# A local-attention and three-way-maximum MLP kernel: chunks of rows in another order, tap sums of two chunks on TensorE, and a new opening list

## The chip, the cores and the metric

The kernel runs on one core of a Trainium2 chip. The core has five engines that run beside each other, each in its own program order: TensorE (PE in the profile; its weight loads are PEld), VectorE (DVE), ScalarE (ACT), GpSimd (POOL) and SyncE (SP), which in this kernel issues every DMA. The metric is the device time of one execution in microseconds (us). One profiled execution gives the trace; times inside it are counted from the start of its span.

## The reference

Inputs are x (8 x 4160 x 192), weight_gen (8 x 4160 x 8 heads x 7 taps), w1, w2, w3 (192 x 768) and w_out (768 x 192), as 64-bit words for the four matrices. With S positions in a sequence:

```python
w = exp(weight_gen - max over taps); w = w / (sum over taps + 1e-9)
x_pad = 6 zero rows, then x                       # for each of the 8 sequences
attn[s, h] = sum over k of w[s, h, k] * x_pad[s + k, h]      # 24 columns for a head
h = max(max(attn @ w1, attn @ w2), attn @ w3)
out = h @ w_out
```

All float32. Each position needs the six rows before it in its own sequence; at the start of a sequence these are zeros.

## The kernel before

The 33280 positions lie on 128 partitions, 260 consecutive positions (t) on each; a sequence fills 16 partitions. A chunk is four values of t, so 4 x 128 = 512 positions, and there are 65 chunks. A chunk at t = a needs the rows a - 6 to a + 3, so the chunks at t = 0 and t = 4 need rows that belong to the partition before; these come first in this kernel, as chunks 0 and 1. Chunks are loaded in groups ("supers": chunk 0, chunk 1, then threes), by `load_super`: one DMA for the tap weights (wt) and one for the rows (xt), with two buffers of each. Where rows of the partition before are needed, the load is three DMAs, and `clear` on VectorE or `clear_by_dma` (a copy out of a stretch of zeros in `ident`) wipes the rows that a first partition of a sequence must not see.

For each chunk:

- softmax over the taps (`softmax`, L195), once for a super.
- `product` (L220): for each of its four t, GpSimd multiplies seven shifted rows by their weights into r (128 x 192 x 7, taps innermost, three buffers).
- `total` (L240): VectorE adds the seven taps into acc.
- `transpose` (L251): acc is turned so that the 192 columns lie on partitions. For the first three chunks (ON_TENSOR) TensorE does it, with two transposes for each t, into PSUM; for all others VectorE and ScalarE.
- `parts` (L277): the turned x is split into a high part in TensorE's fast 32-bit format and the remainder: xa_hi, xa_lo (columns 0 to 127) and xb, xc (columns 128 to 191 and their remainder).
- `up` (L323): the three products with w1, w2, w3 for six blocks of 128 hidden columns. One matmul uses half of the array's rows (64 partitions), and two streams, "half 0" and "half 1", run on the two halves beside each other. After half 0 of a step SP gets a `nop` that waits for it, and half 1 of the same step waits for that nop (L320, `after`): SP is a relay, in its program order between its DMAs.
- `maximum` (L341): ScalarE copies the first product to m, VectorE takes the maximum with the other two, ScalarE makes h_hi and GpSimd h_lo = m - h_hi.
- `down` (L370): h times w_out, four pieces, one chunk late; the output DMA follows.

The matrices arrive as 64-bit words and are turned into 32-bit high and low parts by `split`, in units a0 to a5 (rows 0 to 127 of w1, w2, w3, two blocks of hidden columns at a time), b0 to b2 (rows 128 to 191) and d0 to d2 (w_out). For a b unit a copy with exchanged partition halves is needed too ("the swap", L566): for b0 and b1 by two DMAs each from wb_hi to wb_hi, for b2 by ScalarE. Blocks 0 and 1 of the hidden columns need b0, blocks 2 and 3 need b1.

The order of the opening is a table, OPENING: at each tick (22 ticks are a chunk) a list of stages, such as x0.3 (product of chunk 0, t = 3), +0.3 (its sum), t0 (the next piece of chunk 0's transpose), p0 (parts), s1 (softmax of super 1), a0, b0, d0 (the next stage of a unit). LOADS gives the order of the first loads. Later work goes by fixed ticks, with `load_super` of a later super issued at tick 5 of the chunk five before its first.

Of the kernel before, what the change touches and what calls it, by code (L numbers as in the profile page):

```python
# [13 lines left out]
F32 = mybir.dt.float32  # L14
F32R = mybir.dt.float32r
U32 = mybir.dt.uint32
U16 = mybir.dt.uint16
I32 = mybir.dt.int32
AF = mybir.ActivationFunctionType
ALU = mybir.AluOpType  # L20
AX = mybir.AxisListType
# [1 line left out]
P = 128  # L23
# [51 lines left out]
UNITS_D = ((0, 2), (2, 4), (4, 6))  # L75
SIGN_ON_VECTOR = ()
# [4 lines left out]
def lightconv_maxout_kernel(  # L81
# [61 lines left out]
    inside = edges[:, 4:5].bitcast(I32)  # L143
# [10 lines left out]
    def load_super(s):  # L154
        cs = supers[s]
        a = chunks[cs[0]][0]
        n = sum(chunks[c][1] for c in cs)
        xt = sup.tile([P, TS + PAD, D], F32, name="xt")
        wt = sup.tile([P, TS, H * K], F32, name="wt")
        pin(nc.sync.dma_start(out=wt[:, :n], in_=wf[:, a : a + n]))  # L160
        if a >= PAD:
            pin(nc.sync.dma_start(out=xt[:, : n + PAD], in_=xf[:, a - PAD : a + n]))
        else:


            z = PAD - a
            rows = x.rearrange("b s d -> (b s) d")[NT - z : P * NT - z]
            rows = rows.rearrange("(p t) d -> p t d", t=NT)[:, : n + PAD]
            for p, q in ((PB, P), (1, PB)):
                pin(nc.sync.dma_start(out=xt[p:q, : n + PAD], in_=rows[p - 1 : q - 1]))  # L170
            pin(nc.sync.dma_start(out=xt[:1, z : n + PAD], in_=xf[:1, : a + n]))
            if s == 0:
                pin(nc.vector.memset(xt[:1, :z], 0.0))
        state["x", s], state["w", s], state["n", s] = xt, wt, n

    def clear(s):

        n = PAD // 2
        for t in (n, 0):
            xs = state["x", s][:, t : t + n].rearrange("p t d -> p (t d)").bitcast(I32)  # L180
            pin(
                nc.vector.tensor_tensor(
                    xs, xs, inside.broadcast_to([P, n * D]), op=ALU.bitwise_and
                )
            )
            yield

    def clear_by_dma(s, n):
        c = 4 * G
        xt = state["x", s][:, :n].rearrange("p t d -> p (t d)")  # L190
        xt = xt.rearrange("(b q) (r c) -> b q r c", q=PB, c=c)[:, 0]
        zeros = ident[:B, P - c :].unsqueeze(1).broadcast_to([B, n * D // c, c])
        pin(nc.sync.dma_start(out=xt, in_=zeros))
# [26 lines left out]
    def product(c, t):  # L220

        s = super_of[c]
        a, n = chunks[c]
        la = a - chunks[supers[s][0]][0]
        xt, wt = state["x", s], state["w", s]
        r = att.tile([P, D, K], F32, name="r", bufs=3)
        state["r", c, t] = r
        pin(
            nc.gpsimd.tensor_tensor(  # L229
                r.rearrange("p (h g) k -> p k h g", g=G),  # L230
                xt[:, la + t : la + t + K].rearrange("p k (h g) -> p k h g", g=G),
                wt[:, la + t]
                .rearrange("p (h k) -> p k h", k=K)
                .unsqueeze(3)
                .broadcast_to([P, K, H, G]),
                op=ALU.mult,
            )
        )

    def total(c, t):  # L240

        r = state.pop(("r", c, t))
        if ("acc", c) not in state:
            state["acc", c] = att.tile([P, TC, D], F32, name="acc")
        pin(
            nc.vector.tensor_reduce(  # L246
                state["acc", c][:, t], r, axis=AX.X, op=ALU.add
            )
        )

    def transpose(c):  # L251

        acc = state["acc", c]
        if c < ON_TENSOR:
            pa, pb = (ps.tile([P, CH], F32, name="ph") for _ in range(2))
            pb = pb[:DB]
            state["p", c] = pa, pb
            for t in range(TC):
                to = slice(t * P, (t + 1) * P)
                pin(nc.tensor.transpose(pa[:, to], acc[:, t, :P], ident))  # L260
                pin(nc.tensor.transpose(pb[:, to], acc[:, t, P:], ident))  # L261
# [79 lines left out]
    def maximum(step, odd):  # L341

        c, jp, i = step
        N = chunks[c][1] * P
        j = 2 * jp + odd
        if jp == 0 and i == 0 and odd == 0:
            state["h", c] = (
                hp.tile([P, NJ, CH], F32R, name="h_hi"),
                hp.tile([P, NJ, CH], F32R, name="h_lo"),
            )  # L350
        h_hi, h_lo = state["h", c]
        ph = state.pop(("ph", step, odd))
        if i == 0:
            state["m", j] = mp.tile([P, CH], F32, name="m", bufs=4)
        m = state["m", j]
        if i == 0:
            pin(nc.scalar.copy(m[:, :N], ph[:, :N]))  # L357
        else:
            pin(nc.vector.tensor_tensor(m[:, :N], ph[:, :N], m[:, :N], op=ALU.max))  # L359
        if i == 2:  # L360
            hi, lo = h_hi[:, j, :N], h_lo[:, j, :N]
            later(1, lambda: pin(nc.scalar.copy(hi, m[:, :N])))  # L362
            later(
                2,
                lambda: pin(
                    nc.gpsimd.tensor_tensor(lo, m[:, :N], hi.bitcast(F32), op=ALU.subtract)  # L366
                ),
            )

    def down(c, t, js, half):  # L370
# [163 lines left out]
                in_=w[:P, 4 * jp * P : 4 * (jp + 1) * P],  # L534
            )

    def load_rest():
        for i, w in enumerate(words[:3]):
            for odd, h in enumerate(halves):
                nc.sync.dma_start(  # L540
                    out=raw_b[h, :, i].rearrange("p j n w -> p j (n w)"),
                    in_=w[P:].rearrange("p (j o n) -> p j o n", j=NJ // 2, o=2)[:, :, odd],
                )

    def load_down():
# [60 lines left out]
    def stage(name):  # L606

        c, *t = map(int, name[1:].split("."))
        if name[0] == "x":
            finish(f"s{super_of[c]}")  # L610
            if c == 0 and t[0] == PAD // 2:
                if "c0" not in running:
                    stage("c0")
            elif c == 0:
                finish("c0")
# [15 lines left out]
    def finish(name):  # L631
# [103 lines left out]
```

## Time and profile before

| | |
|---|---|
| median of 3 runs | 1685.53 us (1685.09 to 1685.88) |
| the profiled execution's own time | 1685.41 us |
| its span in the trace | 1683.6 us |
| VectorE busy | 1109.6 us, 66% |
| ScalarE busy | 1136.8 us, 68% |
| GpSimd busy | 1418.9 us, 84% |
| DMA | 79.95 MB, mean 47 GB/s; the first of 40 slices moves 226 GB/s |

How to read it: "busy" is the share of the span in which an engine has an instruction under way. A matmul's end is modelled, so an engine that is always busy may still have slack; where an engine waits, the trace names what released it. "SPq" is SP's queue, which issues DMAs and relays. A DMA's landing is the time from its issue to the arrival of its last bytes.

### The profile page before, as it was taken

The numbers are of one execution on the slowest core, as the hardware profiler recorded it, in microseconds if no ns is written. First come the engines' busy times: TensorE is split into PE (matmuls) and PEld (weight loads), VectorE is DVE, ScalarE is ACT, GpSimd is POOL, SyncE is SP. The second block draws the span as 40 slices with busy tenths as digits, with TensorE's granted clock in tenths as the row PEclk, the third lists the DMA queues.
The fourth block names the chain that finished last, engine by engine and source line by source line (L and its number), as shares of the span: only waits on it lengthen the run. The fifth ranks groups of instructions, "written<-read, shape, count | busy, mean of one in ns | idle before, by whom it ended". The sixth has DMA issues, their size and how long they took to land.

```text
span 1683.6 us, 42090 instructions
## 1 busy us (share of the span) xinstructions
PE 1651.1 (98%) x16794; PEld 1640.7 (97%) x16794; DVE 1109.6 (66%) x1504; ACT 1136.8 (68%) x2862; POOL 1418.9 (84%) x834
## 2 busy tenths in 40 slices
PE   3999999999999999999999999999999999999999
PEld 2899999999999999999999999999999999999999
DVE  8866666666666666666666666666666666666653
ACT  6566676676676676676676676676676676676672
POOL 7977988888888888888888888888888888888862
PEclk9999999999999999999999999999999999999999
DMA  7110101011010101011010101011010101010000
GB/s 226 54 67 20 65 16 70 20 62 70 20 62 20 71 11 70 21 61 71 20 61 21 70 11 70 20 62 70 20 62 20 70 11 70 20 62 20 21 11 29
DMA packets 20333, 79.95 MB, mean 47 GB/s; under 512 B 2216, under 2 KB 5160, under 8 KB 17448
## 3 DMA queue, kind: packets, MB, share of 16 engines
q1 hardware_dynamic: 20136, 77.27, 12.3%
q8 instruction: 131, 2.15, 0.5%
q14 instruction: 66, 0.54, 0.1%
HBM read 51.29 MB, written 25.56 MB: 46 GB/s over the span
## 4 chain that ended last, share of the span: by engine, by line
PE 98%; DMA 1%; DVE 0%; ACT 0%; issue 0%; SPq 0%
PE ph L309 97%; DMA h_hi<-in_moe_w_dram 0%; DMA xt<-in_x_dram 0%; DMA h_lo<-in_moe_w_dram 0%; DVE ph L484 0%; DVE ph L491 0%; ACT ph L457 0%; ACT low L459 0%; PE ph L260 0%; ACT low L463 0%; ACT xc L290 0%; PE ph L261 0%; DVE red L200 0%; DVE acc L246 0%; DVE ph L468 0%
## 5 line engine op out<-in xcount | busy, mean ns | idle before, releaser
L229 POOL TENSOR_TENSOR r<-xt,wt 128x1344 f32<-128x1344 f32 x260 | 722.6, 2821 | 6.9 <-DMA xt<-ident 3.6
L359 DVE TENSOR_TENSOR m<-ph,m 128x512 f32<-128x512 f32 x780 | 520.5, 685 | 204.3 <-PE ph L309 118.5
L366 POOL TENSOR_TENSOR h_lo<-m,h_hi 128x512 fp32r<-128x512 f32 x390 | 503.2, 1302 | 164.5 <-ACT h_hi L362 159.7
L309 PE MATMUL ph<-xa_hi,wa_hi 64*128 64x512 f32 x2340 | 623.3, 389 | 3.0 <-DVE w L491 1.9
L309 PE MATMUL ph<-xa_lo,wa_hi 64*128 64x512 f32 x2340 | 621.1, 387 | 0.6 <-DVE xa_lo L288 0.6
L309 PE MATMUL ph<-xb,wb_hi 64*128 64x512 f32 x2340 | 621.0, 387 | 0.3 <-ACT wb_hi L505 0.3
L309 PE MATMUL ph<-xa_hi,wa_lo 64*128 64x512 f32 x2340 | 621.2, 387 | 0.0
L309 PE MATMUL ph<-wo,h_hi 64*128 64x384 f32 x3120 | 591.7, 355 | 0.0
L309 PE MATMUL ph<-wo,h_lo 64*128 64x192 f32 x3120 | 551.8, 247 | 0.0
L362 ACT CAST h_hi<-m 128x512 fp32r<-128x512 f32 x390 | 242.1, 621 | 421.8 <-DVE m L359 418.7
L246 DVE TENSOR_REDUCE acc<-r 128x192 f32<-128x1344 f32 x260 | 401.7, 1547 | 124.6 <-POOL r L229 124.6
L309 PEld LDWEIGHTS ph<-wo,h_lo 64*128 64x128 f32 x3120 | 458.6, 188 | 0.0
L274 ACT COPY room<-room 32x128 f32<-32x128 f32 x1488 | 440.7, 296 | 22.9 <-DVE room L268 4.7
L309 PE MATMUL ph<-xc,wb_lo 64*128 64x512 f32 x1170 | 452.4, 387 | 1.7 <-POOL wb_lo L508 1.7
L309 PEld LDWEIGHTS ph<-wo,h_hi 64*128 64x128 f32 x3120 | 453.7, 184 | 0.0
L309 PEld LDWEIGHTS ph<-xa_hi,wa_hi 64*128 64x128 f32 x2340 | 358.0, 184 | 5.7 <-ACT ph L457 2.6
L309 PEld LDWEIGHTS ph<-xa_lo,wa_hi 64*128 64x128 f32 x2340 | 357.4, 185 | 2.1 <-DVE xa_lo L288 1.1
L309 PEld LDWEIGHTS ph<-xb,wb_hi 64*128 64x128 f32 x2340 | 357.3, 184 | 2.0 <-ACT wb_hi L505 0.8
L309 PEld LDWEIGHTS ph<-xa_hi,wa_lo 64*128 64x128 f32 x2340 | 357.3, 184 | 1.5 <-issue 0.4
L357 ACT COPY m<-ph 128x512 f32<-128x512 f32 x390 | 222.0, 586 | 40.7 <-PE ph L309 32.2
L392 DVE TENSOR_TENSOR o<-ph,ob 128x192 f32<-128x192 f32 x260 | 86.5, 353 | 232.9 <-ACT ob L391 232.9
L309 PEld LDWEIGHTS ph<-xc,wb_lo 64*128 64x128 f32 x1170 | 215.7, 184 | 2.8 <-POOL wb_lo L508 2.2
(78 smaller groups left out, 666.6 us busy)
## 6 DMA issues: line engine op xcount, KB each, us to landing
xt<-in_x_dram SPq DMA_DIRECT2D x21, 1728.0 KB, 7.0
out_dram<-o SPq DMA_DIRECT2D x64, 384.0 KB, 2.3
wt<-in_weight_gen_dram SPq DMA_DIRECT2D x21, 336.0 KB, 3.0
xt<-in_x_dram SPq DMA_DIRECT2D x2, 840.0 KB, 7.4
h_hi<-in_moe_w_dram SPq DMA_DIRECT2D x6, 256.0 KB, 7.2
h_lo<-in_moe_w_dram SPq DMA_DIRECT2D x6, 192.0 KB, 5.8
room<-in_moe_w_out_dram SPq DMA_DIRECT2D x1, 1152.0 KB, 7.0
raw_a<-in_moe_w_dram SPq DMA_DIRECT2D x3, 256.0 KB, 7.0
```

The lines of the kernel that those rows point to most:

```text
L229: nc.gpsimd.tensor_tensor(r.rearrange("p (h g) k -> p k h g", g=G), xt[:, la + t : la + t + K].rearrange("p k (h g) -> p k h g", g=G), wt[ ...
L246: nc.vector.tensor_reduce(state["acc", c][:, t], r, axis=AX.X, op=ALU.add)
L274: pin(nc.scalar.copy(to[:, :, p : p + 32], blocks[p : p + 32, :, f : f + 32]))
L309: ins = nc.tensor.matmul(ph[:, :n], w[h], v[h], start=begins and half == 0 and q == 0, stop=ends and half == 1 and q == len(terms) - 1,)
L357: pin(nc.scalar.copy(m[:, :N], ph[:, :N]))
L359: pin(nc.vector.tensor_tensor(m[:, :N], ph[:, :N], m[:, :N], op=ALU.max))
L362: later(1, lambda: pin(nc.scalar.copy(hi, m[:, :N])))
L366: nc.gpsimd.tensor_tensor(lo, m[:, :N], hi.bitcast(F32), op=ALU.subtract)
L392: pin(nc.vector.tensor_tensor(o[:, t], po[:, :D], ob, op=ALU.add))
```

## The change

Six things change:

1. The chunks are taken from t = 12 on, and the chunks at t = 0, 4 and 8 come last, as one super (chunks 62 to 64). `load_super` of that super clears six rows with a VectorE memset and issues ten DMAs: wt, xt, and for each of the eight sequences one of 15 partitions x 6 rows. `clear`, `clear_by_dma` and what they need go.
2. For the eight t of chunks 0 and 1 (ADD_ON_TENSOR) GpSimd writes r with the taps outermost, VectorE's sum is left out, and TensorE transposes all seven taps into the same PSUM place, adding them: 14 transposes for each t instead of two.
3. For ten pairs of chunk and block (H_LO_ON_VECTOR, chunks 0 to 3) the third maximum is written in place in PSUM, and VectorE instead of GpSimd makes h_lo.
4. The loads come in another order, the b matrices in two pieces: "s0 a0 b0 a2 b12 s1 a1 d".
5. All twelve units use the shorter of the two ways through `split` (WHOLE); LO_ON_POOL and HI_ON_VECTOR name other units.
6. The list OPENING is new.

```diff
+    0: "b1 s1 a5 b2 a5 b1 b2",
+    1: "+1.2 +1.0 b1 a2 b2 a3 a2 a3 a2 s2 a3 a2 b2 b2 d0",
+    5: "a2 a3 d0 a3 d2 s1 d0 t1",
+    6: "s0 x0.2 d0 a3 s2 +0.1 d0 d1 d2 s2 s0 d2 d1 a3 a5 d1 d1 p1 d1 b1 b0 +1.1 d2",
...
+ADD_ON_TENSOR = ("x0.0", "x0.1", "x0.2", "x0.3", "x1.0", "x1.1", "x1.2", "x1.3")
-LO_ON_POOL = ("a4", "b0", "b2", "d0")
+LO_ON_POOL = ("a2", "a4", "a5", "b1", "d0")
 BY_DMA = ("b0", "b1")
-HI_ON_VECTOR = ("d2",)
-WHOLE = ("a0", "a1", "a2", "a4", "b1", "b2")
+H_LO_ON_VECTOR = ("h0.0", "h0.1", "h0.2", "h0.4", "h0.5", "h1.0", "h2.3", "h2.5", "h3.3", "h3.5")
+HI_ON_VECTOR = ("a0",)
+WHOLE = ("a0", "a1", "a2", "a3", "a4", "a5", "b0", "b1", "b2", "d0", "d1", "d2")
-LOADS = "s0 a0 b s1 a1 a2 d"
+LOADS = "s0 a0 b0 a2 b12 s1 a1 d"
...
     chunks = [(t, TC) for t in range(0, NT, TC)]
+    chunks = chunks[SC:] + chunks[:SC]
...
             z = PAD - a
-            for p, q in ((PB, P), (1, PB)):
-                pin(nc.sync.dma_start(out=xt[p:q, : n + PAD], in_=rows[p - 1 : q - 1]))
-            pin(nc.sync.dma_start(out=xt[:1, z : n + PAD], in_=xf[:1, : a + n]))
+            pin(nc.vector.memset(xt[:, :z], 0.0))
+            pin(nc.sync.dma_start(out=xt[:, z : n + PAD], in_=xf[:, : a + n]))
+            for b in range(B):
+                to = slice(b * PB + 1, (b + 1) * PB)
+                pin(
+                    nc.sync.dma_start(
+                        out=xt[to, :z], in_=xf[to.start - 1 : to.stop - 1, NT - z :]
+                    )
+                )
...
+        if f"x{c}.{t}" in ADD_ON_TENSOR:
+            r = r.rearrange("p (k f) -> p k f", k=K)
+            to = r.rearrange("p k (h g) -> p k h g", g=G)
+            ready(c).append(t)
...
+                for k, part in enumerate(parts):
+                    for po, f in ((pa, slice(0, P)), (pb[:DB], slice(P, D))):
+                        pin(
+                            nc.tensor.matmul(
+                                po[:, t * P : (t + 1) * P],
+                                part[:, f],
+                                ident,
+                                is_transpose=True,
+                                start=k == 0,
+                                stop=k == len(parts) - 1,
+                            )
+                        )
...
+        in_place = i == 2 and f"h{c}.{j}" in H_LO_ON_VECTOR
+        to, eng = (ph, nc.vector) if in_place else (m, nc.gpsimd)
+        pin(nc.vector.tensor_tensor(to, ph, m, op=ALU.max))
```

Where instructions stand in SP's queue in the opening, before the change. The names: room is where w_out's raw words land, wt and xt are a super's loads (128x672 and 128x3456 for a super of three chunks), wb_hi<-wb_hi are the swaps of b0 and b1.

```order
L532 DMA h_hi<-in_moe_w_dram 128x512 x3
L532 DMA raw_a<-in_moe_w_dram 128x512 x3
L546 DMA room<-in_moe_w_out_dram 128x6x384
L193 DMA xt<-ident 8x4x96
L160 DMA wt<-in_weight_gen_dram 128x672
L162 DMA xt<-in_x_dram 128x3456
L566 DMA wb_hi<-wb_hi 64x384 x4
L160 DMA wt<-in_weight_gen_dram 128x672
L162 DMA xt<-in_x_dram 128x3456
L400 DMA out_dram<-o 128x768 x2
```

The same place in SP's queue after the change.

```order
L155 DMA wt<-in_weight_gen_dram 128x224
L157 DMA xt<-in_x_dram 128x1920
L539 DMA h_hi<-in_moe_w_dram 128x512 x3
L554 DMA room<-in_moe_w_out_dram 128x6x384
L155 DMA wt<-in_weight_gen_dram 128x672
L157 DMA xt<-in_x_dram 128x3456
L574 DMA wb_hi<-wb_hi 64x384 x2
L155 DMA wt<-in_weight_gen_dram 128x672
L157 DMA xt<-in_x_dram 128x3456
L574 DMA wb_hi<-wb_hi 64x384 x2
L407 DMA out_dram<-o 128x768 x2
```

The four swaps stood together between the loads of super 2 and super 3; now the two of b0 stand there, and the two of b1 stand behind the loads of super 3.

The end of SP's queue before the change: the loads of the last super and the outputs.

```order
L160 DMA wt<-in_weight_gen_dram 128x672
L162 DMA xt<-in_x_dram 128x3456
L400 DMA out_dram<-o 128x768 x3
L160 DMA wt<-in_weight_gen_dram 128x672
L162 DMA xt<-in_x_dram 128x3456
L400 DMA out_dram<-o 128x768 x8
L396 DMA out_dram<-o 128x192 x4
```

And after the change.

```order
L407 DMA out_dram<-o 128x768 x3
L155 DMA wt<-in_weight_gen_dram 128x672
L161 DMA xt<-in_x_dram 128x2304
L165 DMA xt<-in_x_dram 15x1152 x8
L407 DMA out_dram<-o 128x768 x8
L403 DMA out_dram<-o 128x192 x4
```

Two loads in a row have become ten, the last of which waits until the landing count that it shares with the xt load is free (eight such counts go round).

GpSimd's queue in the opening after the change, from chunk 0's products (128x1344, taps outermost) to chunk 1's last; before, all products of the two chunks were 128x7x192 with VectorE's sums behind them.

```order
L212 TENSOR_TENSOR r<-xt,wt 128x1344 x4
L178 TENSOR_TENSOR wt<-wt,red 128x224
L515 TENSOR_TENSOR wa_lo<-w,wa_hi 128x2x2x128
L515 TENSOR_TENSOR wa_lo<-w,wa_hi 128x2x128
L191 TENSOR_TENSOR wt<-wt,den 128x224
L212 TENSOR_TENSOR r<-xt,wt 128x1344 x2
L178 TENSOR_TENSOR wt<-wt,red 128x672
L212 TENSOR_TENSOR r<-xt,wt 128x1344 x2
L515 TENSOR_TENSOR wb_lo<-w,wb_hi 128x384
```

With three buffers of r, the fourth of chunk 1's products now waits until TensorE has transposed the first of them; on TensorE these 14 transposes stand after the matmuls of blocks 0 and 1 have begun, 28 matmuls on, counted from the first one that reads a swapped half of b0.

More of the change, by code (lines that the diff above doesn't have):

```diff
@@ L17 @@
 U16 = mybir.dt.uint16
-I32 = mybir.dt.int32
 AF = mybir.ActivationFunctionType
@@ L142, in lightconv_maxout_kernel @@
     over, span, below, warm = (edges[:, k : k + 1] for k in range(4))
-    inside = edges[:, 4:5].bitcast(I32)
     F_MAX = float(np.array((E_MIN + E_MAX) << 16 | 0xFFFF, np.uint32).view(np.float32))
@@ L166, in load_super @@
             z = PAD - a
-            rows = x.rearrange("b s d -> (b s) d")[NT - z : P * NT - z]
-            rows = rows.rearrange("(p t) d -> p t d", t=NT)[:, : n + PAD]
-            for p, q in ((PB, P), (1, PB)):
-                pin(nc.sync.dma_start(out=xt[p:q, : n + PAD], in_=rows[p - 1 : q - 1]))
-            pin(nc.sync.dma_start(out=xt[:1, z : n + PAD], in_=xf[:1, : a + n]))
-            if s == 0:
-                pin(nc.vector.memset(xt[:1, :z], 0.0))
-        state["x", s], state["w", s], state["n", s] = xt, wt, n
[L176 to L193, printed above, removed]
+            pin(nc.vector.memset(xt[:, :z], 0.0))
[7 more added lines that the diff above has]
+                )
+        state["x", s], state["w", s], state["n", s] = xt, wt, n
     def softmax(s):
@@ L225, in product @@
         xt, wt = state["x", s], state["w", s]
-        r = att.tile([P, D, K], F32, name="r", bufs=3)
+        r = att.tile([P, D * K], F32, name="r", bufs=3)
+        if f"x{c}.{t}" in ADD_ON_TENSOR:
+            r = r.rearrange("p (k f) -> p k f", k=K)
+            to = r.rearrange("p k (h g) -> p k h g", g=G)
+            ready(c).append(t)
+        else:
+            r = r.rearrange("p (f k) -> p f k", k=K)
+            to = r.rearrange("p (h g) k -> p k h g", g=G)
         state["r", c, t] = r
@@ L238, in product, with ready @@
         )
+    def ready(c):
+        return state.setdefault(("ready", c), [])
     def total(c, t):
+        if f"x{c}.{t}" in ADD_ON_TENSOR:
+            return
+        ready(c).append(t)
         r = state.pop(("r", c, t))
@@ L251, in transpose @@
     def transpose(c):
-        acc = state["acc", c]
         if c < ON_TENSOR:
[L255 to L261, printed above, removed]
+            for n in range(TC):
+                if n == len(ready(c)):
+                    finish("+{}.{}".format(c, min(set(range(TC)) - set(ready(c)))))
+                if n == 0:
+                    pa, pb = (ps.tile([P, CH], F32, name="ph") for _ in range(2))
+                    state["p", c] = pa, pb[:DB]
+                t = ready(c)[n]
+                if f"x{c}.{t}" in ADD_ON_TENSOR:
+                    r = state.pop(("r", c, t))
+                    parts = [r[:, k] for k in range(K)]
+                else:
+                    parts = [state["acc", c][:, t]]
+                for k, part in enumerate(parts):
[10 more added lines that the diff above has]
+                        )
                 yield
             return
+        acc = state["acc", c]
         v = xtp.tile([P, NJ * D * 2], F32, name="room", bufs=1)
@@ L354, in maximum @@
             state["m", j] = mp.tile([P, CH], F32, name="m", bufs=4)
-        m = state["m", j]
+        m = state["m", j][:, :N]
+        ph = ph[:, :N]
         if i == 0:
-            pin(nc.scalar.copy(m[:, :N], ph[:, :N]))
-        else:
-            pin(nc.vector.tensor_tensor(m[:, :N], ph[:, :N], m[:, :N], op=ALU.max))
+            pin(nc.scalar.copy(m, ph))
+            return
+        in_place = i == 2 and f"h{c}.{j}" in H_LO_ON_VECTOR
+        to, eng = (ph, nc.vector) if in_place else (m, nc.gpsimd)
+        pin(nc.vector.tensor_tensor(to, ph, m, op=ALU.max))
         if i == 2:
             hi, lo = h_hi[:, j, :N], h_lo[:, j, :N]
-            later(1, lambda: pin(nc.scalar.copy(hi, m[:, :N])))
+            later(1, lambda: pin(nc.scalar.copy(hi, to)))
             later(
[L364 to L367, printed above, removed]
+                2, lambda: pin(eng.tensor_tensor(lo, to, hi.bitcast(F32), op=ALU.subtract))
             )
@@ L535, in load_up, with load_rest @@
             )
-    def load_rest():
+    def load_rest(js):
+        js = slice(int(js[0]), int(js[-1]) + 1)
         for i, w in enumerate(words[:3]):
@@ L540, in load_rest @@
                 nc.sync.dma_start(
-                    out=raw_b[h, :, i].rearrange("p j n w -> p j (n w)"),
-                    in_=w[P:].rearrange("p (j o n) -> p j o n", j=NJ // 2, o=2)[:, :, odd],
+                    out=raw_b[h, js, i].rearrange("p j n w -> p j (n w)"),
+                    in_=w[P:].rearrange("p (j o n) -> p j o n", j=NJ // 2, o=2)[:, js, odd],
                 )
@@ L588, in lightconv_maxout_kernel @@
             load_up(int(name[1:]))
+        elif name[0] == "b":
+            load_rest(name[1:])
         else:
-            {"b": load_rest, "d": load_down}[name]()
+            load_down()
     make_identity(nc, ident)
-    clear_by_dma(1, PAD - TC)
     NC = len(chunks)
@@ L610, in stage @@
             finish(f"s{super_of[c]}")
[L611 to L615, printed above, removed]
         elif name[0] == "+":
@@ L619, in stage @@
             done[name] = done.get(name, 0) + 1
-            for t in range(min(done[name], TC) if c < ON_TENSOR else TC):
-                finish(f"+{c}.{t}")
+            if c >= ON_TENSOR:
+                for t in range(TC):
+                    finish(f"+{c}.{t}")
         elif name[0] == "p":
@@ L636, in lightconv_maxout_kernel @@
         "s": softmax,
-        "c": clear,
         "x": product,
```

9 lines of the change are left out of this document (3 added, 6 removed), and 35 rows, old and new, of the table OPENING.

## The prediction

> **What bounds the kernel now.** I read the page first, then the chain of work that ended last, then TensorE's timeline in the opening, then SP's queue.
>
> ```profile
> PE 1651.1 (98%) x16794; PEld 1640.7 (97%) x16794; DVE 1109.6 (66%) x1504; ACT 1136.8 (68%) x2862; POOL 1418.9 (84%) x834
> PE 98%; DMA 1%; DVE 0%; ACT 0%; issue 0%; SPq 0%
> 36.51 8.94 PE ph L309 x62
> 62.32 1617.56 PE ph L309 x15710
> ```
>
> TensorE is busy 98% of the span and 97% of the chain is its matmuls (first two rows: page and chain). The last two rows, from the chain in order of time, say where the slack is: from 36.5 us on the matmuls run without a gap to the end, the last 1617.56 us of it in one piece. So nothing in VectorE, ScalarE or GpSimd is worth anything by itself. What counts is when the unbroken stream starts, what is added to TensorE's own queue, and whether something new interrupts the stream.
>
> ```profile
> 26.66 0.79 PE L309 MATMUL ph<-xa_hi,wa_hi 64*128 64x512 f32 x1 [1.12 <-ACT xa_hi L284]
> 36.51 0.80 PE L309 MATMUL ph<-xa_hi,wa_hi 64*128 64x512 f32 x2 [1.91 <-DVE w L491]
> 38.38 1.02 PE L309 MATMUL ph<-xa_hi,wa_hi 64*128 64x512 f32 x2
> 38.81 1.02 PE L309 MATMUL ph<-xa_lo,wa_hi 64*128 64x512 f32 x2
> ...
> 41.19 0.60 PE L309 MATMUL ph<-xa_hi,wa_hi 64*128 64x512 f32 x2
> 41.42 0.59 PE L309 MATMUL ph<-xa_lo,wa_hi 64*128 64x512 f32 x2
> ...
> 43.70 0.58 PE L309 MATMUL ph<-xb,wb_hi 64*128 64x512 f32 x2
> ```
>
> In TensorE's timeline (start, length, what, idle before and its releaser) the first real matmul comes at 26.66, a last gap of 1.91 us ends at 36.51. Up to about 39.7 us the pairs start 0.43 us apart, from then on 0.23: the clock is at half speed for the first 3.4 us of the stream, which costs 1.7 us. I use the row at 43.70 as a landmark: by the program's order it holds the first matmul that reads a swapped half of b1.
>
> **What the change does to the stream, step by step.** The swaps first, since TensorE waits for them.
>
> ```profile
> 20.39 0.74 SPq L193 DMA_DIRECT2D xt<-ident  x1
> 21.24 0.37 SPq L160 DMA_DIRECT2D wt<-in_weight_gen_dram  x1
> 21.71 0.38 SPq L162 DMA_DIRECT2D xt<-in_x_dram  x1
> 29.13 2.47 SPq L566 DMA_DIRECT2D wb_hi<-wb_hi  x4
> 27.14 2.65 POOL L229 TENSOR_TENSOR r<-xt,wt 128x1344 f32<-128x1344 f32 x1 [3.58 <-DMA xt<-ident]
> DMA to landing us min/median/max: 6.7/7.0/10.8
> DMA to landing us min/median/max: 2.4/2.7/3.1
> ```
>
> The rows are SP's issues in the opening, GpSimd's wait for the small copy out of ident, and the landing times of the loads of L162 and of the swaps of L566. The copy out of ident is 12 KB, was issued at 20.39 and released GpSimd only at 27.14: it lay behind the w_out load issued just before it. A later DMA of this queue thus lands behind the bytes in front of it. The first L162 load (super 2), issued at 21.71, has the longest landing, 10.8 us, so it is in at 32.5; the loads up to there carry the same bytes before and after. After the change the two swaps of b0 stand right behind this load as before, and land 0.2 us apart after it (estimate, from the last swap: issued at 31.0, landing at least 2.4 later, 33.4 for the fourth), so at about 33.1.
>
> ```profile
> 8.34 1.43 DVE L182 TENSOR_TENSOR xt<-xt,edges 128x576 int32<-128x576 int32 x2 [2.95 <-DMA xt<-in_x_dram]
> 9.24 8.08 POOL L229 TENSOR_TENSOR r<-xt,wt 128x1344 f32<-128x1344 f32 x3 [3.12 <-DVE xt L182]
> L246 DVE TENSOR_REDUCE acc<-r 128x192 f32<-128x1344 f32 x260 | 401.7, 1547 | 124.6 <-POOL r L229 124.6
> ```
>
> TensorE needs them at its eighth real matmul. Everything earlier is hidden behind that wait: chunk 0's 56 transposes, its parts, its weights. Chunk 0's rows land at 8.3 (first row: VectorE's clear waits for them); without the clear GpSimd's four products, 2.7 each (second row), end near 19, the last transposes 3 us later at half clock, and ScalarE's parts by about 25 (estimate). So the stream restarts at 33.1 instead of 36.5, with a cold clock again. That the eight sums on VectorE and the clears are gone cannot be seen in it, and the units' shorter way and new places neither; this cover of some 8 us holds against misses of a few us, and where it were gone each late us would be one of the result.
>
> ```profile
> 45.06 0.39 PE L309 MATMUL ph<-xa_hi,wa_lo 64*128 64x512 f32 x1
> ...
> 61.50 0.27 PE L260 MATMUL ph<-ident,acc 128*128 128x128 f32 x1
> 61.61 0.27 PE L261 MATMUL ph<-ident,acc 128*64 128x128 f32 x1
> L229 POOL TENSOR_TENSOR r<-xt,wt 128x1344 f32<-128x1344 f32 x260 | 722.6, 2821 | 6.9 <-DMA xt<-ident 3.6
> xt<-in_x_dram SPq DMA_DIRECT2D x21, 1728.0 KB, 7.0
> wt<-in_weight_gen_dram SPq DMA_DIRECT2D x21, 336.0 KB, 3.0
> ```
>
> A transpose costs 0.11 us of TensorE (61.50 to 61.61). Chunk 1 has 56 of them in the stream instead of 8, which is 48 x 0.11 = 5.3 us more, if nothing else were waited for. But something is: the swaps of b1 now stand behind super 3's loads, and these wait for chunk 1's last product, whose weights lie in the buffer that they overwrite. That product waits for a buffer of r, which TensorE frees with chunk 1's first 14 transposes. From 33.1: 28 matmuls take 5.2 us (before, the 28 from 36.51 on end near 41.4, 4.9 us; after the restart the second half-stream joins late, so a little more), the 14 transposes 1.5, to 39.8; the product 2.8 (2821 ns), to 42.6; wt issue 0.4, then xt lands 7.0 after its issue, at 50.0, and the swaps 0.4 to 0.9 later. I take **50.8** for the landmark. TensorE itself would be there at 33.1 + 7.7 (matmuls: 7.2 before, from 36.51 to 43.70, and again a little more) + 6.1 (56 transposes) = 46.9, so it stands still for some 3.9 us, and the 5.3 us lie inside the 50.8. Landmark: 50.8 - 43.7 = **+7.1**. The old kernel still has its eight transposes of chunk 1 ahead at that point, the new one not: **-1.0** (45.06, the matmul ahead of them, to 46.4 is 1.3 us, less one step of 0.23).
>
> ```profile
> SPq L320 <- PE ph L309: 1567.9, 1435, 4.3
> 2.15 0.22 SPq L171 DMA_DIRECT2D xt<-in_x_dram  x1
> 1472.24 0.34 SPq L160 DMA_DIRECT2D wt<-in_weight_gen_dram  x1
> 1472.63 0.42 SPq L162 DMA_DIRECT2D xt<-in_x_dram  x1
> ```
>
> The last super's ten DMAs are the third place. SP relays half 0 to half 1: 1435 waits for TensorE (first row, SP's waits), one for every 1.1 us of the stream. In before a super takes SP 0.8 us (1472.24 to 1473.05). Now SP issues wt, xt and seven small ones, at 0.22 to 0.42 each, then waits for xt's landing before the tenth. xt is 1152 KB: in a usual super 1728 KB land 7.0 + 0.4 - 3.0 = 4.4 us after wt, so 1152 KB take 2.9, and xt is in 5.5 us after its issue. SP is away for 0.4 + 5.5 + 0.3 = 6.2 us. TensorE has one to two relays in hand, I take 1.9 us: **+4.3** stall. Bounds: 1 us, if nothing but ten issues at 0.22 counts; 6 us, if xt takes the full 7.0.
>
> ```profile
> 1679.90:1681.70 1.80, 0.00 (x0) 0.00 (x0) 0.49 (x2) 0.32 (x1) 0.00 (x0) 1.00 0.60 192
> 1681.80:1683.60 1.80, 0.00 (x0) 0.00 (x0) 0.00 (x0) 0.00 (x0) 0.00 (x0) 0.50 0.02 6
> ```
>
> Both stalls may drop the clock. In these two stretches at the end of before TensorE has nothing to do from 1679.9 on, and the granted clock (the number ahead of the DMA share) is 0.50 by 1681.8: under 2 us of idleness were enough. A stall of 4 us should do, and costs half of some 3.4 us as at the start: **+1.7 each, +3.4**; bounds 0 and 2.4 each.
>
> The Trainium skill, TensorE: Matmul & The Clock Gate, Part 1, has the gate watch free-running windows of about 3.4 us, open after a busy one and close after at least one idle one. The opening agrees on the first (3.4 us). On closing the end of the trace differs, since less than 2 us of idleness sufficed; by the page's rule a stall of 4 us would seldom hold a whole window, and the sum would be 3.4 lower, 1695.8.
>
> ```profile
> L366 POOL TENSOR_TENSOR h_lo<-m,h_hi 128x512 fp32r<-128x512 f32 x390 | 503.2, 1302 | 164.5 <-ACT h_hi L362 159.7
> ```
>
> The other edits cost nothing: ten h_lo go from GpSimd (1302 ns) to VectorE, which has just lost eight sums of 1547 ns, and both have idle time under the stream. The last super's rows come five chunks early. For the products' new layout the trace has no row; taken as 2821 ns. A product 0.6 faster would move the landmark by 0.6; a slower one by as much.
>
> Sum: 7.1 - 1.0 + 4.3 + 3.4 = +13.8 us. The profiled execution took 1685.41 for a span of 1683.6, so 1.8 lie around it, and it stands 0.1 below the median. 1685.4 + 13.8 = 1699.2; I say **1699**.
>
> **The rivals.**
>
> (a) One of the two stalls is short or the clock stays up: the sum without the 3.4, or without the last super's 4.3 + 1.7, is 1693 to 1696. For it: a relay is a small thing, and TensorE may have more in hand. Against: relays stand in program order behind the DMAs.
>
> (b) The other side, not slower: swaps do not wait for the bytes ahead, and land 2.7 us (median row) after their issue. This decides from one point, whether the first lands before 30. Then the weights set the start: of VectorE's eight sums five lay ahead of 36.5, 5 x 1.5 = 7.7, less 1 for the clamps that VectorE takes over with a3 and b0 (estimate), some 29.8. That is -6.7; the clock is up by then, -1.7; by the program's order 18 matmuls more are done by then, 0.11 each, -2.0; the transposes +5.3; the landmark's stall is gone, the last super's 6.0 stays. Together +1, 1686.5; without that stall too, 1680, which is faster. Against: the ident row. The Trainium skill, DMA: Bandwidth & Descriptors, section on queues, rings and completion order, says that completion is not first-in-first-out for an issuing engine. That would be this case. The same section has each engine take descriptors in ring order, and the ident row bears this out.
>
> (c) Worse: a transpose that adds costs more than 0.11, or the clock comes back later: 1703 and above. Some 0.07 more each (3.9 us over 56) is swallowed by the wait for the swaps.
>
> (d) The change doesn't do what it says, because VectorE's sums were what held the start: they were (the row at 36.51 names VectorE), but the swaps are due 3 us earlier at best, so the gain is 3 us and not 7. That is in the sum.
>
> **How the numbers follow.** Forecast 1696 to 1703: 0.62. (a) 0.16. (b) 0.12 near 1686.5, and 0.06 below 1682. (c) 0.04. The range 1687 to 1703 takes in (a) and part of (b); the forecast's own is 1696 to 1703. 0.2% is 3.4 us, about what a measurement of this kernel can tell from no change: faster 0.06, same 0.12, slower 0.82.
>
> **What would show it.** In the trace after: TensorE idle from about 25 to 33 with the swap's DMA as releaser; a second gap of about 4 us ending near 51, again at wb_hi; a third of about 4 us some eight chunks before the end, ended by SP; pairs 0.43 us apart behind each. I am wrong if the swaps land before super 2's load, or if the stream is unbroken from 34 us on.

## The result, and the profile after

| | before | after |
|---|---|---|
| median (lowest to highest) | 1685.36 (1685.09 to 1685.88) | 1701.39 (1699.38 to 1701.97) |
| profiled execution, its span | 1685.41, 1683.6 | 1699.38, 1697.2 |

Four runs each; the ratio is 1.0093, 95% interval 1.0075 to 1.011. The change makes the kernel 0.9% slower, 16.0 us by the medians and 13.6 us between the two profiled spans. The forecast was 1699, from +13.8 us on the span.

First the page of after: busy time and three groups of instructions, of which the last two numbers are the idle time of the engine just before them and what ended most of it.

```profile
PE 1666.8 (98%) x16890; PEld 1597.0 (94%) x16890; DVE 1106.3 (65%) x1507; ACT 1130.2 (67%) x2850; POOL 1406.7 (83%) x824
L316 PE MATMUL ph<-xb,wb_hi 64*128 64x512 f32 x2340 | 797.2, 388 | 9.4 <-DMA wb_hi<-wb_hi 9.4
L316 PE MATMUL ph<-xa_hi,wa_hi 64*128 64x512 f32 x2340 | 800.8, 390 | 5.0 <-SPq L327 4.2
L212 POOL TENSOR_TENSOR r<-xt,wt 128x1344 f32<-128x1344 f32 x260 | 720.0, 2812 | 9.1 <-PE ph L259 8.1
```

The shares of TensorE look like those of before; the loss does not show in a percentage. It shows in the idle columns: 9.4 us in which TensorE waited for a transfer into wb_hi (the swaps), 4.2 us in which it waited for SP (the relay, now L327), and GpSimd's 8.1 us for TensorE's transposes. The chain of after, in order of time (start, length, what), puts these in a row:

```profile
13.93 6.55 DMA xt<-in_x_dram
20.50 10.97 DMA wb_hi<-wb_hi
...
31.51 6.08 PE ph L316 x28
37.59 1.69 PE ph L259 x14
...
39.42 2.58 POOL r L212
43.59 6.55 DMA wb_hi<-wb_hi
...
50.18 18.68 PE ph L316 x148
...
69.89 1408.72 PE ph L316 x13721
...
1479.15 5.64 DMA xt<-in_x_dram
1484.81 0.40 SPq L165
...
1485.32 208.42 PE ph L316 x1990
```

The one piece of before (62.32 us to the end) is cut at 1479, and ahead of it stands a loop through four engines: matmuls, 14 transposes that free a buffer of r, GpSimd's product, SP's loads of super 3, and the swaps of b1 that land behind those loads. TensorE's timeline has the three gaps in the brackets, and SP's queue what it did in the last one:

```profile
31.51 0.79 PE L316 MATMUL ph<-xb,wb_hi 64*128 64x512 f32 x1 [6.39 <-DMA wb_hi<-wb_hi]
50.18 0.70 PE L316 MATMUL ph<-xb,wb_hi 64*128 64x512 f32 x1 [3.01 <-DMA wb_hi<-wb_hi]
1485.32 0.79 PE L316 MATMUL ph<-xa_hi,wa_hi 64*128 64x512 f32 x1 [4.24 <-SPq L327]
1478.76 0.34 SPq L155 DMA_DIRECT2D wt<-in_weight_gen_dram  x1
1479.15 0.42 SPq L161 DMA_DIRECT2D xt<-in_x_dram  x1
1481.74 3.47 SPq L165 DMA_DIRECT2D xt<-in_x_dram  x8
SPq L165 <- DVE xt L160: 2.1, 1, 2.1
```

SP is away from 1478.76 to 1485.21. Ahead of the first small load it waits 2.1 us for VectorE's memset of xt (last row, from SP's waits). The eight small loads then take 3.47 us, which is what eight issues of 0.40 with 0.04 between them take, and the relay behind them ends TensorE's pause. The chain names xt's landing at 1484.79 (1479.15 + 5.64), since that fell 0.02 us ahead of the eighth issue; SP's waits show no wait for it in this execution. What the pauses do to the clock is read in stretches (start:end, length, busy time and instructions of PE, PEld, DVE, ACT and POOL, granted clock, DMA share, GB/s):

```profile
31.50:36.60 5.10, 5.09 (x24) 4.08 (x26) 0.00 (x0) 0.59 (x1) 0.00 (x0) 0.50 0.00 0
...
50.40:53.70 3.30, 3.30 (x18) 2.56 (x18) 1.98 (x3) 1.17 (x2) 3.01 (x2) 0.50 0.00 0
53.80:57.00 3.20, 3.20 (x32) 2.61 (x30) 1.41 (x2) 0.59 (x1) 0.00 (x0) 1.00 0.02 5
1483.90:1490.70 6.80, 5.38 (x26) 4.25 (x28) 2.83 (x3) 1.91 (x5) 4.11 (x3) 0.50 0.28 78
```

Half clock stands behind each pause: 5.1 us of stream from 31.51, 3.4 from 50.3, 5.4 from 1485.32. The first of these stretches began at 23.0 already, ahead of the wait for b0's swaps. A stretch at half clock costs half its length.

### The profile page after: what moved, and what is told of

Its sections match the earlier page's. It is cut to its first block, busy times and chain, and to the rows that moved or that the text cites. A ratio compares the mean times of both kernels' runs of the same rounds, so it can differ in the third digit from the quotient of the medians.

```text
span 1697.2 us, 42279 instructions
## 1 busy us (share of the span) xinstructions
PE 1666.8 (98%) x16890; PEld 1597.0 (94%) x16890; DVE 1106.3 (65%) x1507; ACT 1130.2 (67%) x2850; POOL 1406.7 (83%) x824
## 4 chain that ended last, share of the span: by engine, by line
PE 97%; DMA 2%; SPq 1%; POOL 0%; issue 0%; DVE 0%; ACT 0%; POOLq 0%
PE ph L316 97%; DMA wb_hi<-wb_hi 1%; DMA xt<-in_x_dram 1%; DMA h_hi<-in_moe_w_dram 0%; SPq L548 0%; PE ph L259 0%; POOL r L212 0%; SPq L155 0%; SPq L539 0%; SPq L157 0%; SPq L574 0%; SPq L165 0%; DVE o L399 0%; ACT ob L398 0%; SPq L327 0%
## 5 line engine op out<-in xcount | busy, mean ns | idle before, releaser
L316 PE MATMUL ph<-xb,wb_hi 64*128 64x512 f32 x2340 | 797.2, 388 | 9.4 <-DMA wb_hi<-wb_hi 9.4
L316 PE MATMUL ph<-xa_hi,wa_hi 64*128 64x512 f32 x2340 | 800.8, 390 | 5.0 <-SPq L327 4.2
L316 PE MATMUL ph<-xa_lo,wa_hi 64*128 64x512 f32 x2340 | 796.5, 388 | 2.3 <-DVE xa_lo L295 2.3
L316 PE MATMUL ph<-xa_hi,wa_lo 64*128 64x512 f32 x2340 | 796.5, 388 | 0.0
L374 POOL TENSOR_TENSOR h_lo<-m,h_hi 128x512 fp32r<-128x512 f32 x380 | 490.5, 1302 | 181.1 <-ACT h_hi L372 176.2
L316 PE MATMUL ph<-wo,h_hi 64*128 64x384 f32 x3120 | 608.1, 355 | 0.0
L316 PEld LDWEIGHTS ph<-xb,wb_hi 64*128 64x128 f32 x2340 | 418.4, 185 | 24.7 <-DMA wb_hi<-wb_hi 10.5
L316 PEld LDWEIGHTS ph<-xa_hi,wa_hi 64*128 64x128 f32 x2340 | 418.9, 185 | 20.2 <-SPq L327 4.8
L316 PEld LDWEIGHTS ph<-xa_lo,wa_hi 64*128 64x128 f32 x2340 | 419.0, 185 | 16.4 <-DVE xa_lo L295 2.6
L316 PEld LDWEIGHTS ph<-xa_hi,wa_lo 64*128 64x128 f32 x2340 | 418.5, 185 | 14.8 <-issue 0.2
```

The costliest lines, as they stand in the source:

```text
L316: ins = nc.tensor.matmul(ph[:, :n], w[h], v[h], start=begins and half == 0 and q == 0, stop=ends and half == 1 and q == len(terms) - 1,)
L374: 2, lambda: pin(eng.tensor_tensor(lo, to, hi.bitcast(F32), op=ALU.subtract))
```

## The experiments

All were timed against the kernel before on the same chip (its medians there: 1685.25 for e1 to e4, 1685.65 for e5 to e7, 1685.97 for e8 to e10).

| run | edit | median (lowest to highest) | ratio to before, 95% |
|---|---|---|---|
| e1 | after, small loads spread | 1693.43 (1692.9 to 1693.98) | 1.0047 [1.0032, 1.0062] |
| e2 | after, super 3's loads later | 1695.11 (1694.81 to 1696.64) | 1.0056 [1.0039, 1.0073] |
| e3 | after, swaps on ScalarE's queue | 1698.96 (1697.23 to 1700.06) | 1.0079 [1.0064, 1.0094] |
| e4 | after, swaps copied by ScalarE | 1688.05 (1687.01 to 1689.88) | 1.0015 [1.0006, 1.0025] |
| e5 | e1 and e4 | 1681.72 (1680.21 to 1682.36) | 0.9976 [0.9967, 0.9986] |
| e6 | e1, loads behind the swaps | 1683.97 (1682.27 to 1685.37) | 0.9990 [0.9981, 0.9999] |
| e7 | e5, chunk 1 summed on VectorE | 1686.53 (1685.84 to 1688.04) | 1.0004 [0.9995, 1.0013] |
| e8 | e5, filler transposes | 1679.99 (1679.58 to 1681.64) | 0.9968 [0.9956, 0.9980] |
| e9 | e5, h_lo back on GpSimd | 1695.95 (1694.76 to 1696.46) | 1.0059 [1.0046, 1.0071] |
| e10 | before, swaps copied | 1686.65 (1685.83 to 1689.3) | 1.0006 [0.9997, 1.0015] |

### e1: the small loads spread

```diff
-                pin(nc.sync.dma_start(out=xt[to, :z], ...))
+                later(2 + 2 * b, lambda to=to: pin(nc.sync.dma_start(out=xt[to, :z], ...)))
```

> Only the eight small loads of the last super move: one every second tick instead of all eight at once, so that SP's relays come between them. Theory (SP is away from its relays): the gap of 4.24 us at 1481 goes, and with it the 5.4 us of half clock behind it (2.7 us), so some 6.9 us less than the changed kernel's 1701.4: 1694.5, between 1693 and 1696. Rival (the pause comes from VectorE's memset or from the bytes of the load itself): the gap stays, 1701.

1693.43, 8.0 us less than after's median. The third gap is gone, the other two stay (6.12 and 3.18 us). The chain's last long piece, which was broken in two in after, runs from 71.42 on without a break:

```profile
71.42 1616.42 PE ph L319 x15462
```

The third place thus cost what was claimed, and a little more. The edit takes the small loads away from the memset and from xt's landing at once, so it does not tell which of the two held SP.

### e2: super 3's loads two ticks later

```diff
-  at(max(TICKS * (cs[0] - LOAD[0]) + LOAD[1], 0), lambda s=s: load_super(s))
+  at(max(TICKS * (cs[0] - LOAD[0]) + LOAD[1], 0) + 2 * (s == 3), lambda s=s: load_super(s))
```

> Only super 3's two loads move, from tick 5 to tick 7, behind the swaps of b1 in SP's queue. Theory (a swap lands behind the bytes issued before it): b1's swaps land right behind b0's, near 32, the gap of 3.01 us at 47 goes and the 3.4 us of half clock behind it (1.7 us), so some 4.7 us less than 1701.4: 1696.7, between 1695 and 1698.5. Rival (the gap is held by something else that is late near 50, for instance chunk 1's last product): 1701.

1695.11, 6.3 us less. In the DMA issues (KB each, median us to landing) of this run's stretch from 40 to 60 us b1's swaps, now ahead of super 3's load, take 2.1 us; the gap near 47 and its cold clock are gone. They did not land near 32, as expected: SP came to them only at 42.84. In after they landed 6.55 us after their issue, right behind that load. The profiled execution is the slowest of this run's four (1696.64); its stream restarts at 34.61, 3.1 us later than that of after, in a part of the program that the edit leaves as it was.

```profile
wb_hi<-wb_hi SPq DMA_DIRECT2D x2, 96.0 KB, 2.1
```

### e3: the swaps on a queue of their own

```diff
-                pin(nc.sync.dma_start(out=other[to].bitcast(F32), in_=hi[h].bitcast(F32)))
+                pin(nc.scalar.dma_start(out=other[to].bitcast(F32), in_=hi[h].bitcast(F32)))
```

> Only the queue of the swaps changes: ScalarE issues them instead of SP. Theory (order holds within one queue): they land 2 to 4 us after their issue although SP's loads are still under way, the first real gap ends near 27 instead of 31.5, the gap at 47 goes, and less half clock is paid (up to 4.3 us): some 9 to 12 us less than 1701.4, so 1689.5 to 1692.5. Rival (the DMA engines serve all queues in the order of issue): they land near 31 as now, and only the gap at 47 may go: 1696 to 1701.

A miss: 1698.96 instead of 1689.5 to 1692.5, with all three gaps (5.46, 3.10 and 4.59 us). I had taken SP's queue for what the swaps wait in. The rows are ScalarE's issues, then the DMA issues of the stretch from 18 to 22 us, then (from the DMA view of 20 to 34 us) the busy tenths of the 16 DMA engines in 40 slices:

```profile
20.92 1.14 ACTq L574 DMA_DIRECT2D wb_hi<-wb_hi  x2
45.72 0.48 ACTq L574 DMA_DIRECT2D wb_hi<-wb_hi  x1
...
wb_hi<-wb_hi ACTq DMA_DIRECT2D x2, 96.0 KB, 9.2
...
DMA  9999999999999999999999999999882110000000
```

On their own queue b0's swaps still take 9.2 us, while all 16 engines are busy with SP's bytes until about 30. They wait for the engines, which both queues share, and not only for their place in a queue. b1's are issued late in addition (45.72), since ScalarE comes to them in its own order.

### e4: the swaps by copy

```diff
-BY_DMA = ("b0", "b1")
+BY_DMA = ()
```

> Only the means of the swaps changes: ScalarE copies the halves (0.51 us each, four of them) and no DMA is used. Theory: as in the run with their own queue, 1689.5 to 1692.5, since nothing but the landing held TensorE. Rival (the weights or chunk 1's products are late near 31 anyway): the first gap ends near 30 and the gain is 5 us at most, 1696.

1688.05, 13.3 us less than after and more than expected; it is the clean form of what e3 meant to try. Two casts of ScalarE, about 0.5 us each, replace each pair of swaps (first row), both early gaps are gone, and only SP's remains (second row):

```profile
26.05 1.03 ACT L576 CAST wb_hi<-wb_hi 64x384 fp32r<-64x384 f32 x2
1474.46 0.79 PE L316 MATMUL ph<-xa_hi,wa_hi 64*128 64x512 f32 x1 [4.23 <-SPq L327]
```

### e5: e1 and e4 together

> The change with two edits together: the last super's eight small loads go out one every second chunk (as in e1), and the swapped halves of b0 and b1 are copied by ScalarE and not by DMA (as in e4). Theory (the change loses only at three places, each by a DMA that stands in front of something in SP's queue): the gains add up. e4's profile has one gap left, 4.23 us, and half clock for 6.8 us behind it (3.4 lost): 1688.05 - 7.6 = 1680.4; by e1's gain of 8.0 it is 1680.1. Expected 1679.5 to 1682, faster than the kernel before by 0.2 to 0.35%, no gap above 0.5 us in TensorE from 25 us to the end. Rival: the change holds a fourth loss that the three gaps cover (the added transposes, the new split of work): then 1683.5 to 1686, no faster than before.

1681.72, in the expected range, and faster than before. Its chain has no wait of TensorE on a DMA or on SP left; the only pause after 25 us is one of 0.19 us at 41.4, and from 41.58 on the matmuls run to the end:

```profile
41.58 17.38 PE ph L319 x147
58.96 1.02 PE ph L262 x8
59.98 1616.40 PE ph L319 x15462
```

So the change's loss is those DMAs, and with them out of the way its shorter start is worth 0.24% (0.14 to 0.33%).

### e6: only the order of DMAs

The small loads as in e1; super 2's loads issued behind b0's swaps, super 3's behind b1's:

```diff
-  at(max(TICKS * (cs[0] - LOAD[0]) + LOAD[1], 0), lambda s=s: load_super(s))
+  at({2: 0.5, 3: 7}.get(s, TICKS * (cs[0] - LOAD[0]) + LOAD[1]), lambda s=s: load_super(s))
```

> The change with nothing but the order of DMAs edited: the last super's eight small loads one every second chunk, super 2's loads issued behind the swaps of b0, super 3's two ticks later, behind the swaps of b1; the swaps stay DMAs on SP's queue. Theory (the swaps are late only because of the bytes issued ahead of them): the swaps of b0 land within 3 to 4 us of their issue, the stream starts where ScalarE's and VectorE's parts of b0 set it, and the time is that of e5 within 2 us: 1680 to 1684. Rival (the DMA path is slow for the swaps in itself, 8 us in the opening whatever stands ahead): TensorE waits for wb_hi until 28 or later, cold clock behind it: 1685 to 1690.

1683.97: the time falls at the edge of the theory's range, but the sub-claim of 3 to 4 us for b0's swaps fails, and the rival's sign came true. In the DMA issues of 17 to 22 us they took 9.7 us, and TensorE waited until 28.16, with the clock at half until 33.2 (rows from SP's queue, the DMA issues, the stretches, and TensorE's timeline):

```profile
17.19 0.56 SPq L557 DMA_DIRECT2D room<-in_moe_w_out_dram  x1
17.86 1.39 SPq L577 DMA_DIRECT2D wb_hi<-wb_hi  x2
...
room<-in_moe_w_out_dram SPq DMA_DIRECT2D x1, 1152.0 KB, 10.3
wb_hi<-wb_hi SPq DMA_DIRECT2D x2, 96.0 KB, 9.7
...
16.00:22.00 6.00, 2.72 (x20) 1.87 (x17) 5.32 (x15) 4.88 (x11) 4.47 (x6) 1.00 0.97 329
22.00:28.00 6.00, 3.29 (x6) 1.65 (x6) 3.86 (x8) 4.58 (x11) 4.93 (x2) 0.58 1.08 363
...
28.16 0.79 PE L319 MATMUL ph<-xb,wb_hi 64*128 64x512 f32 x1 [1.66 <-DMA wb_hi<-wb_hi]
```

With super 2 behind them the swaps have the next load ahead, w_out's 1152 KB, in at 17.19 + 10.3 = 27.5. The DMA share is 0.97 and 1.08: the opening's bytes fill the engines until then, whoever comes first. TensorE restarts 3.3 us earlier than in after (28.16 instead of 31.51): moving one load saves at most that load's bytes.

### e7: chunk 1 by sums

```diff
-ADD_ON_TENSOR = ("x0.0", "x0.1", "x0.2", "x0.3", "x1.0", "x1.1", "x1.2", "x1.3")
+ADD_ON_TENSOR = ("x0.0", "x0.1", "x0.2", "x0.3")
```

> e5, but chunk 1's taps are summed on VectorE as in before (four sums of 1.55 us) and only the eight transposes of the sums are left to TensorE; chunk 0 keeps its added transposes. Theory A (with no wait left in the stream, the 48 transposes that fall away are worth their time on TensorE, 48 x 0.11 = 5.3 us): 1674.5 to 1677. Theory B (the sums are late: VectorE is busy with parts of b0, b1, b2 and d until about 40 us, the sums must wait behind them, TensorE then waits for chunk 1 and its clock drops): 1683 to 1690. I hold B the likelier, 1687.

1686.53, 4.8 us slower than e5, theory B. 48 transposes fewer, but VectorE is behind. TensorE first waits 2.33 us for a part of the weights (first row), in which the clock drops; VectorE comes to the last two sums only at 39.61, TensorE waits for them (third row), and the clock is at half for 17 us (last row, a stretch):

```profile
31.52 0.79 PE L319 MATMUL ph<-xa_hi,wa_hi 64*128 64x512 f32 x2 [2.33 <-DVE w L501]
39.61 3.01 DVE L239 TENSOR_REDUCE acc<-r 128x192 f32<-128x1344 f32 x2
41.22 0.69 PE L262 MATMUL ph<-ident,acc 128*128 128x128 f32 x2 [3.96 <-DVE acc L239]
31.10:48.00 16.90, 11.75 (x48) 7.38 (x50) 15.02 (x26) 8.64 (x17) 16.82 (x9) 0.50 0.33 127
```

At this place the added transposes thus cost less than the sums that they replace. What they cost by themselves is not shown.

### e8: fillers in the gaps of the start

```diff
+FILL = (13, 20, 0, 6)
...
+            if key == ((0, 0, 0), 0) and half == 0 and q < 4:
+                for _ in range(FILL[q]):
+                    pin(nc.tensor.transpose(spare[:, :P], ident, ident))
             ins = nc.tensor.matmul(
```

> e5 with 39 more transposes of ident into a PSUM tile that nobody reads, placed in TensorE's three idle gaps between chunk 0's last added transpose and the start of the stream (13 ahead of the first matmul, 20 ahead of the second, 6 ahead of the fourth; e5's gaps there are 1.75, 2.42 and 0.46 us, a transpose takes 0.11). They add work and compute nothing. Theory (the half clock from 23.6 to 30.4 in e5 comes from these gaps, and transposes hold the clock up as chunk 0's own seem to have opened it at 13.4): the clock stays at full through the start, and of the 6.0 us that the stream runs at half clock 3.0 come back: 1678 to 1679.5, against 1681.7 of e5. Rival (the clock is opened by matmuls alone, transposes don't count): no change or slightly slower, 1681.5 to 1683, with half clock until about 30 as in e5.

1679.99, 1.7 us below e5, where 2.2 to 3.7 were expected. Against before on their own chips the two ratios are 0.9968 and 0.9976, and their intervals overlap, so the size is not sure. The mechanism is right: of the stretches below the first is e5's and the second this run's, at half and at full clock; the matmuls of one half start 0.43 us apart in e5 and 0.23 here. A part of the missing gain, 0.76 us, is that the faster stream runs into a part of the weights that VectorE has not ready (third row):

```profile
23.70:30.40 6.70, 6.24 (x26) 4.71 (x26) 5.05 (x11) 4.52 (x10) 5.06 (x4) 0.50 0.89 368
23.70:30.40 6.70, 5.94 (x41) 4.24 (x41) 5.13 (x11) 6.36 (x14) 5.13 (x4) 1.00 0.89 362
29.07 0.50 PE L325 MATMUL ph<-xa_hi,wa_hi 64*128 64x512 f32 x2 [0.76 <-DVE w L507]
```

### e9: the ten h_lo back on GpSimd

```diff
-H_LO_ON_VECTOR = ("h0.0", "h0.1", "h0.2", "h0.4", "h0.5", "h1.0", "h2.3", "h2.5", "h3.3", "h3.5")
+H_LO_ON_VECTOR = ()
```

> e5 with the ten h_lo of the opening given back to GpSimd and written from m, as in before (VectorE forms none of them). My prediction costs this edit at nothing, under the cover of VectorE's and GpSimd's idle time. Theory: within 0.7 us of e5, 1681 to 1682.4. Rival (in the opening GpSimd also makes the products of chunk 1 and 2; ten times 1.3 us there delay the chunk 1 products or the down products of chunk 0): TensorE waits for r or h_lo between 30 and 70 us, 2 to 6 us slower, 1684 to 1688.

1695.95, 14.2 us slower than e5: against the theory, in the rival's direction and far beyond its size. The rows are GpSimd's first h_lo and the next products in this run, a later h_lo and the products behind it, the products of the first kind in e5, and TensorE's longest pause in this run:

```profile
43.57 2.65 POOL L377 TENSOR_TENSOR h_lo<-m,h_hi 128x512 fp32r<-128x512 f32 x2 [5.96 <-ACT h_hi L375]
47.62 8.02 POOL L215 TENSOR_TENSOR r<-xt,wt 128x1344 f32<-128x1344 f32 x3
...
70.87 1.30 POOL L377 TENSOR_TENSOR h_lo<-m,h_hi 128x512 fp32r<-128x512 f32 x1 [4.10 <-ACT h_hi L375]
72.12 15.54 POOL L215 TENSOR_TENSOR r<-xt,wt 128x1344 f32<-128x1344 f32 x6
...
39.80 8.21 POOL L215 TENSOR_TENSOR r<-xt,wt 128x1344 f32<-128x1344 f32 x3
...
84.75 0.79 PE L319 MATMUL ph<-xa_hi,wa_hi 64*128 64x512 f32 x1 [6.56 <-DVE m L372]
```

GpSimd, whose queue runs in order, stands 5.96 us at an h_lo whose h_hi ScalarE has not made yet, and the next products come 7.8 us later than in e5. By 72.12 the delay is 13.6 us (e5 starts the same six products at 58.51): seven h_lo stand ahead of them instead of one, 6 x 1.3 = 7.8 us, and the waits for h_hi are 7.2 us longer (5.96 + 4.10 instead of 2.90). TensorE then pauses four times between 50 and 85 us (1.80, 1.42, 1.87 and 6.56 us, 11.7 in all), and the clock drops during the last.

### e10: the copies in the kernel before

The edit of e4, in the kernel before.

> The kernel BEFORE the change, with the one edit of e4: the swapped halves of b0 and b1 are copied by ScalarE and not by DMA. It asks whether e5's gain over before is the change's or the copy's. Theory (in before the stream waits at 36.51 for VectorE, which sums chunk 0; the swaps are in at 33): the copies save nothing, 1685 to 1686.5, same as before. Rival (the swaps were also what held before's start): a start 2 to 3 us earlier, 1682 to 1683.5, and then most of e5's gain has nothing to do with the change.

1686.65, no faster than before. There the start waits for VectorE (in the profile 3.16 us for a part of the weights, until 37.68), not for swaps, so the copy alone is worth nothing there: e5's gain needs the change.

## Why the prediction was right, point by point

| step | predicted | measured |
|---|---|---|
| b0's swaps in, stream restarts | 33.1 | 31.47, 31.51 |
| 28 matmuls, 14 transposes | 5.2 + 1.5 | 6.08 + 1.69 |
| chunk 1's last product ends | 42.6 | 42.00 |
| landmark, stall before it | 50.8 (+7.1), 3.9 | 50.18 (+6.5), 3.01 |
| SP away by the last super, stall | 6.2, 4.3 | 6.45, 4.24 |
| cold clock after the stalls | 1.7 + 1.7 | 1.7 + 2.7 |

With the -1.0 for the eight old transposes, which was not measured by itself, the measured terms add up to 6.5 - 1.0 + 4.2 + 1.7 + 2.7 = 14.1, against 13.6 between the spans.

**The mechanism held at all three places, at the third only in part.** Gaps two and three were each taken away alone: e2 gives back 6.3 us, where the second stall and its cold clock had been put at 3.9 + 1.7 = 5.6, and e1 8.0, where 4.3 + 1.7 = 6.0 had been put for the third. The medians give back more than the terms; by the records 4.24 + 2.7 = 6.9 of the 8.0 is the third gap. In e1's own record the half clock behind the second pause covers 5.9 us of the stream, where after's covers 3.4, so these terms are not the same in each execution. The rest, about 1 us, and the 2.0 us by which after's median lies above its profiled execution (the fastest of its four runs) stay open.

**Two sizes were off, and partly cancelled.** The swaps of b0 landed 1.6 us earlier than 33.1, because super 2's load was in at 31.1 (17.67 + 13.4) and not at 32.5. The 28 matmuls behind them took 0.9 longer, since the clock stayed at half for 5.1 us of stream and not 3.4. The landmark came out 0.6 early. The cold clock after the last stall was mis-sized at 1.7; it was 5.4 us long and cost 2.7.

**At the last super the size was right in part by luck.** The sum had SP wait for xt's landing before its tenth DMA, and had no wait for VectorE's memset. In the profile of after SP waits 2.1 us for that memset and then issues eight loads without a break; the landing falls at the same moment by chance. In e2, e3 and e4 SP shows both waits, 1.9 to 2.0 us for the memset and 0.2 to 0.7 for the landing. By these figures either alone would have ended at about the same time. And SP was away 0.25 us longer than predicted, while TensorE had some 2.3 us of work in hand and not 1.9.

**"A later DMA of this queue lands behind the bytes in front of it"** was right in effect and too narrow in its reason. e3 shows that an own queue is little help while the DMA engines are full, and e6 that in the opening even the place ahead of super 2's load leaves 9.7 us. With idle engines a swap lands in 2.1 us (e2).

**The clock rule.** The prediction took the end of before's trace, where under 2 us of idleness sufficed, against the Trainium skill, TensorE: Matmul & The Clock Gate, Part 1, by whose rule of at least one idle window of about 3.4 us the time would have been 1695.8. The pause of 3.01 us ended with the clock at half at 50.4. On closing the row held for these stalls and the page's rule did not. Under 2 us is not always enough, though: e9's pauses of 1.80, 1.42 and 1.87 us left the clock at full. The clock's stretches at half do agree with the page's window: 3.4 us behind the 3.01 us pause, and twice that, 6.8, from 1483.9 on, inside the 4.24 us one.

**The rivals.** (a) fell: both stalls were there and both dropped the clock. (b) fell as a forecast, but its numbers can be tried: without the early waits it gave 1686.5 (e4: 1688.05), without the last super's stall too 1680 (e5: 1681.72). Its fast side was real; with swaps by DMA the best run was e6's 1683.97. (c) did not happen: 14 transposes took 1.69 us, 0.12 each, and in e7 sums in place of the 48 were slower. (d) was right in that VectorE had held the start. That it was by its sums is argued; e7, where four of them come back, again has TensorE wait for VectorE.

**"The other edits cost nothing"** is true of the sum and hid something. The ten h_lo on VectorE cost nothing there, but e9 shows that, with the order of the changed kernel, 14 us hang on them. The prediction argued from idle time; what counted was the order of GpSimd's queue in the opening, where each h_lo puts back the products behind it by its own length and by its wait for h_hi.

## What to carry to other kernels

Before moving small transfers, list the bytes that every DMA engine still has to move when they are issued, in all queues; a 96 KB transfer that TensorE waits for took 2.1 us on idle engines and 4.5 to 12.6 us behind other loads, and two engine copies of 0.5 us were the better way. An engine that relays between others (SP here) must not issue a burst of DMAs that has to wait for another engine or for a landing: spread over ticks the same eight loads cost nothing that shows. And an instruction on an in-order queue costs its own length and its wait at the head: in e9 the products behind the h_lo came 13.6 us later, by about equal parts of the two, and the kernel took 14 us more.

## What the hardware showed that was not expected

Transposes alone open the clock. In e5 the first 14 transposes take 3.25 us, 0.23 each, and those from 16.70 on 0.12 each, with no matmul before 20.20; and e8's fillers, transposes too, kept the clock at full through the start (there too by the 0.23 us between matmuls). The Trainium skill, TensorE: Matmul & The Clock Gate, Part 4, says that transposes do not engage the full clock; here they did.

```profile
9.14 3.25 PE L262 MATMUL ph<-ident,r 128*128 128x128 f32 x14 [9.14 <-POOL r L215]
16.70 1.75 PE L262 MATMUL ph<-ident,r 128*128 128x128 f32 x14 [0.72 <-POOL r L215]
20.20 0.49 PE L319 MATMUL ph<-xa_hi,wa_hi 64*128 64x512 f32 x1 [1.75 <-ACT xa_hi L294]
```

The granted clock in these views can read 1.00 where the spacing shows half: in before it does so from 36.50 to 39.50, with the pairs 0.43 us apart. In the opening the spacing is the surer sign.

The length of the half clock does not follow from the length of the pause: 3.4 us of the stream behind 3.01 us in after, 5.9 behind 3.18 in e1, 5.4 behind 4.24 in after.
